# Last block's up products in 2x2 blocks: seven block products in place of eight for three pairs of unit tiles

## The chip, the core and the metric

The kernel runs on one core of a Trainium2 chip. A core has a matmul engine (PE, with its weight loads shown apart as PEld), a vector engine (DVE), an activation engine (ACT), GpSimd (POOL) and a queue engine (SP) that issues most DMA transfers. Each engine carries out its own instructions in order; semaphores tie the engines together. The metric is the device time of one execution in microseconds (us), the median of several runs.

## What is computed

Two branches read the same x (2048 rows, 512 columns) and are mixed row by row by a gate g. Branch A is a linear attention with 32 heads of 16; branch B, where the change lies, is a dense layer of 512 to 1376 units, Mish, and a dense layer back.

```python
g = _sigmoid((x * gate_w).sum(-1, keepdims=True))
a = _A_ref(x, A_wqkv, A_w_phi, A_wo)      # hedgehog features, kv and z sums, o @ wo
# branch B
h = jnp.einsum("bsd,df->bsf", x, w1) + b1
sp = jnp.log1p(jnp.exp(-jnp.abs(h))) + jnp.where(h > 0, h, jnp.zeros_like(h))
act = h * jnp.tanh(sp)
b = jnp.einsum("bsf,fd->bsd", act, w2)
return g * a + (1 - g) * b
```

## The kernel before

**Stages.** A first stage (eight chunks of 256 rows) makes k, v and q, the features of k and the sums over rows. The second stage takes four blocks of 512 rows (`b_ops`), numbered 0 to 3 here, the last being the one that the change touches. A block computes branch B, the features of q, the attention output and the final mix.

**Precision by parts.** A float32 operand is kept as a high part (rounded by ACT into a tile of type F32R) and a low part (operand minus high part, by DVE or POOL). A product is three sums of matmuls: high with high, low with high, high with low. With 512 inputs, four tiles of 128, one product of 128 units by 512 rows is 3 x 4 = 12 matmuls of 512 columns into one PSUM bank.

**The steps of a block.** A block's work is a text of step names; `run` carries them out in the order written, and every instruction is pinned, so each engine meets its part in that order. The names that the prediction uses:

- `up{i}`: the 12 matmuls of hidden tile i (11 tiles of 128 units, the order of the tiles in `ORDER`) into one bank of the PSUM tag "a", which has three banks. `mi{i}`: Mish with bias from that bank on ACT. `hi{i}`: the high part on ACT. `lo{i}`: the low part on POOL.
- `dn{i}`: the second layer's 12 matmuls of tile i (three for each 128 rows), into four banks ("dn") that gather all 11 tiles; `df{t}` is the last tile's share for 128 rows t, `fi{t}` the final mix on DVE and the store.
- `T{t}`, `D{t}` ... `tr{t}`: the attention's features of 128 rows, mostly on DVE; `mv{h}`: 16 small transfers on SP; `nu{h}`: 32 narrow matmuls; `oh{h}`, `ol{h}`: high part of their result on ACT and low part on DVE; `wo{t}`, `ag{t}`: the output product and its scaling by the gate on ACT; `ge`, `gg`: the gate. The Exp of `ge` and Mish need different tables, so ACT loads a table (ACT_TABLE_LOAD) between them.
- `XH{j}`, `XL{j}`: high and low part of the next block's x. A `+` behind a name means the next block's step.

Blocks 2 and 3 run in the order of `BLOCK`, block 3 without the steps marked `+`: ... `up4 mi4 hi4 lo4 dn2 up5 mi5 hi5 lo5 dn3 ge gg wo0 ag0 wo1 ag1 up6 mi6 hi6 lo6 dn4 nu1 oh1 ol1 up7 ... dn5 up8 ... dn6 wo2 ag2 wo3 ag3 up9 ... dn7 up10 ... dn8 dn9 df0 fi0 ...`

**Buffers.** Tiles are taken from tags with a fixed number of buffers: "pq" has 3 (2 KB per partition each), "E" 4, "tx" 2 and "z" 1 (4 KB each), "tt" and "eT" 1 (8 KB each). A new tile of a tag waits until the old one in its buffer has been read for the last time. In the second stage "z" holds the attention's z sums, read for the last time by T3 of block 3.

**An earlier use of the same scheme.** `fast_ops` (lines 355 to 402) already computes some of the first stage's k and q in seven products instead of eight, with the copies and sums on ACT and DVE placed between products of other banks.

Of the kernel before, what the change touches and what calls it, by code (L numbers as in the profile page):

```python
# [10 lines left out]
F32R = mybir.dt.float32r  # L11
# [4 lines left out]
P = 128  # L16
# [16 lines left out]
ORDER = [NFA - 1] + list(range(NFA - 1)) + list(range(NFA, NF))
WARM = 6
FAST = range(2, 6)

# [34 lines left out]
BLOCK0 = """  # L71
# [8 lines left out]
BLOCK1 = """  # L80
# [7 lines left out]
BLOCK = """  # L88
# [1 line left out]
    S3 T3 rS3 D3 m3 de3 rd3 sc3 es3 tr3 lq0+ lq1+ mv1 up3 mi3 hi3 lo3 dn1 up4 mi4 hi4 lo4 dn2  # L90
    mx0+ mn0+ d00+ d10+ mx1+ mn1+ d01+ d11+ lq2+ lq3+ up5 mi5 hi5 lo5 dn3 E0+ E1+ ge gg wo0 ag0 wo1 ag1
    S0+ T0+ rS0+ D0+ m0+ de0+ rd0+ sc0+ es0+ tr0+ up6 mi6 hi6 lo6 dn4 nu1 oh1 ol1 S1+ T1+ rS1+ D1+ LX0 LX1 m1+ de1+ rd1+ sc1+
    es1+ tr1+ mv0+ up7 mi7 hi7 lo7 dn5 mx2+ mn2+ d02+ d12+ mx3+ mn3+ d03+ d13+ up8 mi8 hi8 lo8 dn6 E2+ E3+
    wo2 ag2 wo3 ag3 up9 mi9 hi9 lo9 dn7 up10 mi10 hi10 lo10 dn8 XH0+ XL0+ XH1+ XL1+ dn9 df0 fi0 df1 fi1 df2 fi2 df3 fi3
"""


@with_exitstack
def tile_gated_mix(ctx: ExitStack, tc: tile.TileContext, xT, wv, wkT, wqT, bd, w1a, w1b, b1, w2a, w2b, wo, out):
# [6 lines left out]
    pin = tc.keep_in_program_order  # L106
    SYNC = mybir.DependencyInfo(mybir.DependencyClass.Sync, mybir.DependencyReason.DATA)
    V, G_, A_, Sy = nc.vector, nc.gpsimd, nc.scalar, nc.sync

    def mm(*a, **k):  # L110
        return pin(nc.tensor.matmul(*a, **k))  # L111

    def T(shape, dt, tag, bufs, name):
        nm[0] += 1
        return sp.tile(shape, dt, name=f"{name}_{nm[0]}", tag=tag, bufs=bufs)

    def k8(name, tag, dt=F32R):
        return T([P, 2048], dt, tag, 1, name)

    def k4(name, tag, dt=F32):  # L120
        return T([P, 1024], dt, tag, {"E": 4, "tx": 2, "oh": 2, "z": 1}[tag], name)

    def k2(name, tag, dt=F32):
        return T([P, 512], dt, tag, {"pq": 3, "io": 4, "hl": 8}[tag], name)

    def psum(name, tag, bufs={"a": 3, "dn": 4, "kv": 1}):
        nm[0] += 1
        return pp.tile([P, 512], F32, name=f"{name}_{nm[0]}", tag=tag, bufs=bufs[tag])

    def act(out_, in_, fn=AF.Copy, **k):  # L130
        return pin(A_.activation(out_, in_, fn, **k))  # L131

    def kt(t, f):
        return t[:, : KT * f].rearrange("p (k f) -> p k f", f=f)
# [4 lines left out]
    def f32(ap):  # L139
        return ap.bitcast(F32)  # L140
# [39 lines left out]
    ps = psum("warm", "dn")  # L180
# [79 lines left out]
    def feat_ops(key, t, src, d, negative=False):  # L260

        n = str(t)

        def red(name, op):
            d[name] = T([P, H], F32, name, 2, name)
            pin(V.tensor_reduce(d[name], hv(src()), axis=AX.X, op=op))

        def dd(a):
            if "E" not in d:
                d["E"] = k4("E", "E")  # L270
            E = hv(d["E"][:, a * 512 : (a + 1) * 512])
# [21 lines left out]
    def behind(ins, other=None):  # L293
        tc.add_manual_dep(ins.ins, (other or dve[0]).ins.name, SYNC, reason="VectorE's step first")

    def scale_by(d, eng):
        dve[0] = pin(eng.tensor_mul(hv(d["E"][:, :]), hv(d["E"][:, :]), d["S"][:, :, None].to_broadcast([P, 2 * H, DH])))  # L297
# [33 lines left out]
    def fast_operands(c, key):  # L331
# [12 lines left out]
        for j in range(2):  # L344
# [59 lines left out]
    def a_ops(c):  # L404
        key = ("A", c)
        P_ = psA[c] = {}
        for t in range(2):
# [157 lines left out]
    def wo_ops():
        raw = {}
# [25 lines left out]
    B = {}  # L592
# [43 lines left out]
    def b_ops(b):  # L636
        key = ("B", b)
        U, dn, tts, eTs, num, ohl, io = {}, {}, {}, {}, {}, {}, {}

        def up(i):  # L640
            f = ORDER[i]
            xh, xl = xb[b]
            ps = psum("up", "a")
            n = 0
            for w, a in ((0, xh), (1, xh), (0, xl)):
                for k in range(KT):
                    mm(ps, w1_tile(f, w, k), a[:, k, :], start=(n == 0), stop=(n == 3 * KT - 1))
                    n += 1
            U[i] = {"ps": ps}

        def mi(i):
            f = ORDER[i]
            U[i]["a"] = k2("act", "hl")
            act(U[i]["a"], U[i]["ps"], AF.Mish, bias=b1s[:, f : f + 1])

# [8 lines left out]
        def down(i, t):  # L664
            if t not in dn:
                dn[t] = psum("down", "dn")
            f = ORDER[i]
            h, l = [U[i][x][:, t * P : (t + 1) * P] for x in "hl"]
            for n, (a, x) in enumerate(((h, 0), (h, 1), (l, 0))):
                mm(dn[t], a, w2_tile(f, x), start=(i == 0 and n == 0), stop=(i == NF - 1 and n == 2))  # L670

        for i in range(NF):
            at(key, f"up{i}", lambda i=i: up(i))
            at(key, f"mi{i}", lambda i=i: mi(i))
            at(key, f"hi{i}", lambda i=i: hi(i))
            at(key, f"lo{i}", lambda i=i: lo(i))
            for t in range(4):
                at(key, f"dn{i}" if i < NF - 1 else f"df{t}", lambda i=i, t=t: down(i, t))
# [173 lines left out]
    for j in range(2):  # L852
        h, l = [w[:, 2 * j : 2 * j + 2, :].rearrange("p k f -> p (k f)") for w in (wvh, wvl)]
# [12 lines left out]
    for i in range(4):  # L866
        j, r = i // 2, i % 2
# [27 lines left out]
    for c, text in ((NCH - 2, NEXT), (NCH - 1, LAST)):  # L895
        run(text, ("A", c), ("A", c - 1), ("B", 0))
    for b in range(NB):
        run((BLOCK0, BLOCK1, BLOCK, BLOCK)[b], ("B", b), ("B", b - 1), ("B", b + 1))
    assert not steps, list(steps)


# [58 lines left out]
```

## Time and profile before

| | |
|---|---|
| median of 3 runs | 447.92 us (447.35 to 448.15) |
| the profiled execution's own time | 447.83 us |
| its span, first to last instruction | 446.1 us |
| first stage and start of block 0 (0 to 157) | PE busy 154.45 of 157.00 |
| block 3 and the end (369 to 446.1) | PE busy 73.27 of 77.10, DVE 22.14, ACT 22.82, POOL 14.83 |

The span is what the profile covers; the difference to the execution's time lies outside it. A busy time is the sum of an engine's instructions without overlaps counted twice. Matmuls are pipelined: a recorded 0.39 us for a 512-wide one is its whole passage, while the next one starts 0.2267 us later; the distance between starts (the pitch) is what it costs. The chain that ended last goes back from the last instruction, step by step, to whatever released it, and so names the engine that sets the time in each stretch. In rows of timelines the first number is the start in us from the span's start, the second the length, and brackets tell how long the engine stood idle before and what released it.

### The profile page before, as it was taken

To read this page: it belongs to the slowest core of one execution; us is meant where nothing else is said; L and a number is where in the kernel's file an instruction comes from. 1 tells how busy PE (TensorE), PEld (TensorE's weight loads), DVE (VectorE), ACT (ScalarE), POOL (GpSimd) and SP (SyncE) were. 2 spreads that over 40 slices of the span, in tenths; PEclk is the share of its full clock that TensorE was granted. 3 is DMA by queue.
4 is the path that set the end of the run, shared out by engine and by line. 5 is a ranking of instruction groups with operands and counts; after the bars stand their busy time and mean duration, and the time that the engine had idled before them with its cause. 6 is when DMAs were issued, how large, how long until landed. Compare 5 with 4: busy or idle time off the path is not lost.

```text
span 446.1 us, 7022 instructions
## 1 busy us (share of the span) xinstructions
PE 439.7 (99%) x2748; PEld 359.1 (81%) x2748; DVE 319.6 (72%) x427; ACT 211.3 (47%) x292; POOL 158.9 (36%) x120
## 2 busy tenths in 40 slices
PE   7999999999999999999999999999999999999996
PEld 7888888788888888787878887887887888787885
DVE  2499789888999999799899868386967438701002
ACT  5774644463544837426374443724253544234220
POOL 2297388675666364212023121113202123121211
PEclk9999999999999999999999999999999999999999
DMA  7424559949835111405251241321241302030002
GB/s 281 169 77 160 143 122 233 220 130 312 240 116 166 49 24 32 112 19 148 89 171 49 55 134 48 94 96 47 49 143 48 94 2 95 1 91 5 0 0 94
DMA packets 27320, 46.35 MB, mean 104 GB/s; under 512 B 5908, under 2 KB 14100, under 8 KB 27288
## 3 DMA queue, kind: packets, MB, share of 16 engines
q1 hardware_dynamic: 25528, 39.88, 28.9%
q0 software_dynamic: 1616, 5.77, 6.5%
q8 instruction: 21, 0.34, 0.3%
q10 hardware_dynamic: 144, 0.26, 0.2%
q14 instruction: 11, 0.09, 0.1%
HBM read 23.87 MB, written 13.64 MB: 84 GB/s over the span
## 4 chain that ended last, share of the span: by engine, by line
PE 98%; DMA 1%; DVE 0%; issue 0%
PE proj L111 28%; PE up L111 27%; PE down L111 27%; PE wo L111 10%; PE num L111 2%; PE fuse L111 2%; PE kvp L111 2%; DMA bds<-in_bd_dram 1%; DVE io L797 0%; PE z L111 0%; PE kvT L616 0%
## 5 line engine op out<-in xcount | busy, mean ns | idle before, releaser
L662 POOL TENSOR_TENSOR l<-act,h 128x512 fp32r<-128x512 f32 x44 | 60.4, 1373 | 220.5 <-ACT h L131 184.7
L131 ACT ACTIVATE act<-up,b1s 128x512 f32<-128x512 f32 x44 | 30.3, 689 | 87.4 <-PE up L111 87.3
L131 ACT ACTIVATE E<-E 128x1024 f32<-128x1024 f32 x32 | 33.7, 1060 | 47.9 <-DVE E L275 33.8
L297 DVE TENSOR_TENSOR E<-E,Sm 128x1024 f32<-128x1024 f32 x32 | 42.2, 1320 | 1.0
L281 DVE TENSOR_REDUCE Sm<-E 128x64 f32<-128x1024 f32 x32 | 38.7, 1210 | 4.2 <-ACT E L131 4.2
L111 PE MATMUL wo<-woh,ohl 128*128 128x512 f32 x128 | 40.7, 389 | 0.0
L111 PE MATMUL down<-w2ah,h 128*128 128x512 f32 x96 | 37.5, 390 | 0.0
L111 PE MATMUL down<-w2ah,l 128*128 128x512 f32 x96 | 37.4, 389 | 0.0
L111 PE MATMUL down<-w2al,h 128*128 128x512 f32 x96 | 37.3, 389 | 0.0
L797 DVE SCALAR_TENSOR_TENSOR io<-down,og_sb,io 128x512 f32<-128x512 f32 x16 | 11.1, 748 | 31.0 <-PE down L111 31.0
L111 PE MATMUL down<-w2bh,h 128*128 128x512 f32 x80 | 31.2, 390 | 0.0
L111 PE MATMUL down<-w2bl,h 128*128 128x512 f32 x80 | 31.1, 389 | 0.0
L111 PE MATMUL down<-w2bh,l 128*128 128x512 f32 x80 | 31.1, 389 | 0.0
L131 ACT ACT_TABLE_LOAD x20 | 25.7, 1283 | 10.1 <-PE up L111 9.8
L771 DVE TENSOR_TENSOR ohl<-num,ohl 128x512 fp32r<-128x512 f32 x16 | 10.2, 678 | 26.4 <-ACT ohl L131 26.4
L131 ACT ACTIVATE h<-act 128x512 fp32r<-128x512 f32 x44 | 27.8, 632 | 1.4
L111 PEld LDWEIGHTS wo<-woh,ohl 128*128 128x128 f32 x128 | 24.0, 188 | 5.0
L111 PE MATMUL up<-xbh,w1ah 128*128 128x512 f32 x96 | 26.2, 394 | 0.0
L111 PE MATMUL up<-xbh,w1al 128*128 128x512 f32 x96 | 25.7, 389 | 0.0
L111 PE MATMUL up<-xbl,w1ah 128*128 128x512 f32 x96 | 25.7, 389 | 0.0
L559 DVE TENSOR_TENSOR xbl<-xraw,xbh 128x1024 fp32r<-128x1024 f32 x8 | 10.1, 1290 | 21.0 <-ACT xbh L131 21.0
L111 PE MATMUL wo<-wol,ohl 128*128 128x512 f32 x64 | 24.9, 389 | 0.0
(155 smaller groups left out, 1015.3 us busy)
## 6 DMA issues: line engine op xcount, KB each, us to landing
xraw<-in_xT_dram SPq DMA_DIRECT2D x16, 512.0 KB, 4.6
eT<-tt SPq DMA_DIRECT2D x128, 64.0 KB, 2.0
zd<-E POOLq DMA_DIRECT2D x10, 512.0 KB, 7.4
pqd<-qs SPq DMA_DIRECT2D x16, 256.0 KB, 4.0
pq<-pqd SPq DMA_DIRECT2D x16, 256.0 KB, 2.9
out_dram<-io SPq DMA_DIRECT2D x16, 256.0 KB, 2.1
raw<-in_w1a_dram SPq DMA_DIRECT2D x3, 512.0 KB, 4.2
raw<-in_w2a_dram SPq DMA_DIRECT2D x3, 512.0 KB, 3.6
```

The lines of the kernel that those rows point to most:

```text
L111: return pin(nc.tensor.matmul(*a, **k))
L131: return pin(A_.activation(out_, in_, fn, **k))
L281: pin(V.tensor_reduce(d["S"], hv(d["E"][:, :]), axis=AX.X, op=ALU.add))
L297: dve[0] = pin(eng.tensor_mul(hv(d["E"][:, :]), hv(d["E"][:, :]), d["S"][:, :, None].to_broadcast([P, 2 * H, DH])))
L559: dve[0] = pin(V.tensor_sub(xb[b][1][:, :, sl], kt(raw[h], SC), f32(xb[b][0][:, :, sl])))
L662: pin(G_.tensor_sub(U[i]["l"], U[i]["a"], f32(U[i]["h"])))
L771: pin(V.tensor_sub(ohl[h, gp][:, 512:], num[h, gp], f32(ohl[h, gp][:, :512])))
L797: pin(V.scalar_tensor_tensor(io[t], dn[t], og_sb[:, i : i + 1], io[t], op0=ALU.mult, op1=ALU.add))
```

## The change

In block 3 alone, the tiles at places 5 and 6, 7 and 8, 9 and 10 are computed in pairs. A pair is a product of 256 units by 512 rows over 512 inputs; it is cut in two along each (128 units, 256 inputs, 256 rows), and the eight block products are replaced by seven, with sums made before (of x, of w1) and after (of products), as in Winograd's form of Strassen's scheme. `ORDER3` puts neighbouring tiles of w1 side by side in a pair.

```diff
+ORDER3 = [5, 0, 1, 2, 10, 4, 3, 7, 6, 9, 8]
+PAIRS = (5, 7, 9)
@@ BLOCK
-    ... up8 mi8 hi8 lo8 dn6 E2+ E3+
+    ... up8 mi8 hi8 lo8 dn6 E2+ E3+ X1+ Y0+ Y1+ X2+
+BLOCK3 = """
+    up0 mi0 hi0 lo0 gr S2 T2 rS2 D2 m2 de2 rd2 sc2 es2 tr2 up1 mi1 hi1 lo1 up2 mi2 hi2 lo2 dn0 nu0 oh0 ol0
+    S3 T3 LA5 rS3 D3 m3 de3 rd3 sc3 es3 tr3 mv1 LA7 Y2 Y3 up3 mi3 hi3 lo3 dn1 up4 mi4 hi4 lo4 dn2 CA5 HA5 ge gg wo0 ag0 wo1 ag1
+    f1.5 c1.5 f6.5 c6.5 f2.5 f7.5 c7.5 dn3 f5.5 c5.5 f4.5 c4.5 mi5 hi5 lo5 nu1 oh1 ol1 f3.5 c3.5 mi6 hi6 lo6 dn4 CA7 HA7 LA9
+    f1.7 c1.7 f6.7 c6.7 f2.7 f7.7 c7.7 dn5 f5.7 c5.7 f4.7 c4.7 mi7 hi7 lo7 dn6 f3.7 c3.7 mi8 hi8 lo8 CA9 HA9
+    f1.9 c1.9 f6.9 c6.9 f2.9 f7.9 c7.9 dn7 f5.9 c5.9 f4.9 c4.9 mi9 hi9 lo9 dn8 f3.9 c3.9 mi10 hi10 lo10 wo2 ag2 wo3 ag3
+    dn9 df0 fi0 df1 fi1 df2 fi2 df3 fi3
+"""
+    def x_sums(raw, key):
...
+        def x1():
+            pin(G_.tensor_sub(new(0), quarter(0, 1), quarter(0, 0)))
+            pin(G_.tensor_sub(new(1), quarter(1, 1), t[0]))
+            pin(G_.tensor_sub(new(2), quarter(1, 1), quarter(0, 1)))
+        def x2():
+            pin(G_.tensor_sub(new(3), quarter(1, 0), t[1]))
+        def split(i):
+            q = k4("tq", "tx" if i == 3 else "E", F32R)
+            XT[i] = h, l = [q[:, o : o + 512].rearrange("p (k f) -> p k f", k=2) for o in (0, 512)]
+            act(h, t[i])
+            pin(V.tensor_sub(l, t[i], f32(h)))
...
+    def pair_ops(key, n, f0, f1, U):
...
+        def la():
+            r["t"] = k4("wraw", "z")
+            pin(Sy.dma_start(...))
+        def ca():
+            a11, a12, a21, a22 = [...]
+            pin(V.tensor_add(a22, a21, a22))
+            pin(V.tensor_sub(a21, a11, a21))
+            pin(V.tensor_sub(a11, a22, a11))
+            pin(V.tensor_sub(a12, a12, a11))
+        def ha():
...
+            act(hl[0], r["t"])
+            pin(V.tensor_sub(hl[1], r["t"], f32(hl[0])))
...
+        def term(out_, ws, x, start):
+            m = 0
+            for wi, xi in ((0, 0), (1, 0), (0, 1)):
+                for k in range(2):
+                    mm(out_, ws[wi][k], x[xi][:, k, :], start=(start and m == 0), stop=(m == 5), skip_group_check=True)
+                    m += 1
...
+        def c1():
+            c["a"], c["b"] = k2("c", "pq"), k2("c", "pq")
+            act(c["a"][:, lo], ps[0][:, lo])
+        k0, q0, k1, c22 = [lambda i=i, sl=sl: ps[i][:, sl] for i in range(2) for sl in (lo, hi)]
+        p1, e, u2 = lambda: c["a"][:, lo], lambda: c["a"][:, hi], lambda: c["b"][:, lo]
+        for name, fn in (
+            ("f1", f1_), ("c1", c1),
+            ("f6", lambda: term(q0(), w["s2"], XT[1], False)), ("c6", lambda: add(u2, q0, p1)),
+            ("f2", lambda: term(k0(), plain(f0, 1), rows(1, 0), False)),
+            ("f7", f7), ("c7", lambda: add(e, k1, p1)),
+            ("f5", lambda: term(q0(), w["s1"], XT[0], False)), ("c5", lambda: add(c22, q0, e)),
+            ("f4", lambda: term(k1(), plain(f1, 1), XT[3], False)), ("c4", lambda: add(k1, k1, u2)),
+            ("f3", lambda: term(q0(), w["s4"], rows(1, 1), False)), ("c3", lambda: add(q0, q0, p1)),
+        ):
...
         for i in range(NF):
-            at(key, f"up{i}", lambda i=i: up(i))
+            if last and i >= PAIRS[0]:
+                if i in PAIRS:
+                    pair_ops(key, i, tiles[i + 1], tiles[i], U)
+            else:
+                at(key, f"up{i}", lambda i=i: up(i))
...
-        run((BLOCK0, BLOCK1, BLOCK, BLOCK)[b], ("B", b), ("B", b - 1), ("B", b + 1))
+        run((BLOCK0, BLOCK1, BLOCK, BLOCK3)[b], ("B", b), ("B", b - 1), ("B", b + 1))
```

`BLOCK` now serves block 2 alone; the steps `X1+` to `X2+` exist only for block 3's x.

The parts of a pair, named by the place n of its first tile (`f6.7` is f6 of the pair at 7):

- `LA`: one 512 KB transfer of the two raw tiles of w1, into the one buffer of "z". `CA`: four sums of quarters (128 x 2 x 128) on DVE, each in place and all but the first needing the one before. `HA`: their high part (128 x 1024) on ACT, their low part on DVE.
- `f1` to `f7`: six matmuls of 256 columns each. Two banks serve a pair: f1 and f2 write the lower half of the first, f6, f5 and f3 the upper half; f7 and f4 the lower half of the second, and its upper half is written by DVE alone (c5).
- `c1`: a copy of f1's half on ACT (128 x 256). `c6`, `c7`, `c5`, `c4`, `c3`: sums on DVE (128 x 256). `mi` of the pair's first tile reads the second bank after c4, that of its second tile the first bank after c3.
- `X1`, `X2`: four sums of x for the block on POOL (128 x 512), run in the block ahead of it; `Y0` to `Y3`: their high part on ACT and low part on DVE, two in the block ahead, two in block 3.

The order on **PE** from the last pair but one. Names in a row are out<-in; `up_3888` is a bank, xbh and xbl the parts of x, w1bh and w1bl those of w1, tq a sum of x, ws a sum of w1. Before, the step up7, behind nu1:

```order
L111 MATMUL up_3888<-xbh_3521,w1bh_812 128x512 [waits Activation_49]
L111 MATMUL up_3888<-xbh_3521,w1bh_812 128x512 x3
L111 MATMUL up_3888<-xbh_3521,w1bl_813 128x512 x4
L111 MATMUL up_3888<-xbl_3522,w1bh_812 128x512 x4
L111 MATMUL down_3635<-w2ah_128,h_3783 128x512
```

Now f1, f6 and f2 of the pair at 7, behind dn4 (up_3955 is the pair's first bank):

```order
L121 MATMUL up_3955<-xbh_3535,w1bh_812 128x256 [waits Activation_49]
L121 MATMUL up_3955<-xbh_3535,w1bh_812 128x256
L121 MATMUL up_3955<-xbh_3535,w1bl_813 128x256 x2
L121 MATMUL up_3955<-xbl_3536,w1bh_812 128x256 x2
L121 MATMUL up_3955<-tq_3438,ws_3950 128x256 [waits Activation_49]
L121 MATMUL up_3955<-tq_3438,ws_3950 128x256
L121 MATMUL up_3955<-tq_3438,ws_3950 128x256 [waits DVE_49]
L121 MATMUL up_3955<-tq_3438,ws_3950 128x256 x3
L121 MATMUL up_3955<-xbh_3535,w1bh_812 128x256 [waits DVE_49]
L121 MATMUL up_3955<-xbh_3535,w1bh_812 128x256
L121 MATMUL up_3955<-xbh_3535,w1bl_813 128x256 x2
L121 MATMUL up_3955<-xbl_3536,w1bh_812 128x256 x2
```

Where one step of twelve wide matmuls waited once, three steps of six narrow ones now wait four times: for ACT before f1 and before f6, for DVE at f6's third matmul (the low part of the sums of w1) and before f2.

The order on **DVE** behind nu1. Before, the two ol steps, and then nothing until the final mix:

```order
L771 TENSOR_TENSOR ohl_3882<-num_3864,ohl_3882 128x512 [waits Activation_49]
L771 TENSOR_TENSOR ohl_3884<-num_3865,ohl_3884 128x512 [waits Activation_49]
L797 SCALAR_TENSOR_TENSOR io_3816<-down_3635,og_sb,io_3816 128x512 [waits DMAHW6_49,DVE_49,PE_49]
```

Now c4.5, the two ol steps, c3.5, CA7 (lines 623 to 626), HA7's low part (line 635) and c6.7:

```order
L670 TENSOR_TENSOR up_3857<-up_3857,c_3842 128x256 [waits DVE_49,PE_49]
L900 TENSOR_TENSOR ohl_3915<-num_3897,ohl_3915 128x512 [waits Activation_49]
L900 TENSOR_TENSOR ohl_3917<-num_3898,ohl_3917 128x512 [waits Activation_49]
L670 TENSOR_TENSOR up_3834<-up_3834,c_3841 128x256 [waits PE_49]
L623 TENSOR_TENSOR wraw_3722<-wraw_3722 128x2x128 [waits DMAHW5_49]
L624 TENSOR_TENSOR wraw_3722<-wraw_3722 128x2x128 [waits DVE_49]
L625 TENSOR_TENSOR wraw_3722<-wraw_3722 128x2x128 [waits DVE_49]
L626 TENSOR_TENSOR wraw_3722<-wraw_3722 128x2x128 [waits DVE_49]
L635 TENSOR_TENSOR ws_3950<-wraw_3722,ws_3950 128x1024 [waits DMAHW3_49,DMAHW4_49,DMAHW2_49,DMAHW6_49,DMAHW1_49,DMAHW7_49,DMAHW0_49,Activation_49]
L670 TENSOR_TENSOR c_3963<-up_3955,c_3962 128x256 [waits PE_49,Activation_49]
```

The sums for the second pair stand on DVE behind the first pair's last sum (c3.5) and ahead of the second pair's first (c6.7); those for the third pair stand in the same way between c3.7 and c6.9, without the ol steps.

More of the change, by code (lines that the diff above doesn't have):

```diff
@@ L92 @@
     S0+ T0+ rS0+ D0+ m0+ de0+ rd0+ sc0+ es0+ tr0+ up6 mi6 hi6 lo6 dn4 nu1 oh1 ol1 S1+ T1+ rS1+ D1+ LX0 LX1 m1+ de1+ rd1+ sc1+
-    es1+ tr1+ mv0+ up7 mi7 hi7 lo7 dn5 mx2+ mn2+ d02+ d12+ mx3+ mn3+ d03+ d13+ up8 mi8 hi8 lo8 dn6 E2+ E3+
+    es1+ tr1+ mv0+ up7 mi7 hi7 lo7 dn5 mx2+ mn2+ d02+ d12+ mx3+ mn3+ d03+ d13+ up8 mi8 hi8 lo8 dn6 E2+ E3+ X1+ Y0+ Y1+ X2+
     wo2 ag2 wo3 ag3 up9 mi9 hi9 lo9 dn7 up10 mi10 hi10 lo10 dn8 XH0+ XL0+ XH1+ XL1+ dn9 df0 fi0 df1 fi1 df2 fi2 df3 fi3
+"""
[6 more added lines that the diff above has]
+    dn9 df0 fi0 df1 fi1 df2 fi2 df3 fi3
 """
@@ L563, in x_ops, with quarter, new @@
             at(split, f"XL{h}", xl)
+        if b == NB - 1:
+            x_sums(raw, split)
+    XT = {}
+    def x_sums(raw, key):
+        t = {}
+        def quarter(j, r):
+            return kt(raw[r], SC)[:, 2 * j : 2 * j + 2, :]
+        def new(i):
+            t[i] = k2("traw", "pq")[:, :].rearrange("p (k f) -> p k f", k=2)
+            return t[i]
+        def x1():
[9 more added lines that the diff above has]
+            pin(V.tensor_sub(l, t[i], f32(h)))
+        at(key, "X1", x1)
+        at(key, "X2", x2)
+        for i in range(4):
+            at(key, f"Y{i}", lambda i=i: split(i))
@@ new lines, in pair_ops, with quarter, plain, rows @@
+    def pair_ops(key, n, f0, f1, U):
+        n_, dram, g, nf = ("w1a", w1a, f0, NFA) if f0 < NFA else ("w1b", w1b, f0 - NFA, NFB)
+        r, w, c, ps = {}, {}, {}, {}
+        def quarter(t, i, j):
+            return t[:, 2 * j : 2 * j + 2, i, :]
+        def la():
+            r["t"] = k4("wraw", "z")
+            pin(Sy.dma_start(r["t"].rearrange("p (k m) -> p k m", k=KT), dram.rearrange("p (k m) -> p k m", k=KT)[:, :, g * P : (g + 2) * P]))
+        def ca():
+            a11, a12, a21, a22 = [quarter(r["t"][:, :].rearrange("p (k i f) -> p k i f", k=KT, i=2), i, j) for i in range(2) for j in range(2)]
+            pin(V.tensor_add(a22, a21, a22))
[3 more added lines that the diff above has]
+        def ha():
+            if n == PAIRS[0]:
+                hl = k4("wsh", "E", F32R)[:, :], k4("wsl", "tx", F32R)[:, :]
+            else:
+                t = k8("ws", "tt" if n == PAIRS[1] else "eT")
+                hl = t[:, :1024], t[:, 1024:]
+            act(hl[0], r["t"])
+            pin(V.tensor_sub(hl[1], r["t"], f32(hl[0])))
+            v = [x.rearrange("p (k i f) -> p k i f", k=KT, i=2) for x in hl]
+            for name, i, j in (("s2", 0, 0), ("s4", 0, 1), ("s3", 1, 0), ("s1", 1, 1)):
+                w[name] = [[quarter(x, i, j)[:, k, :] for k in range(2)] for x in v]
+        def plain(f, j):
+            return [[w1_tile(f, x, 2 * j + k) for k in range(2)] for x in range(2)]
+        def rows(j, h):
+            return [x[:, 2 * j : 2 * j + 2, h * SC : (h + 1) * SC] for x in xb[NB - 1]]
+        def term(out_, ws, x, start):
[4 more added lines that the diff above has]
+                    m += 1
+        lo, hi = slice(0, SC), slice(SC, RB)
+        def f1_():
+            ps[0] = psum("up", "a")
+            term(ps[0][:, lo], plain(f0, 0), rows(0, 0), True)
+            U[n + 1] = {"ps": ps[0]}
+        def f7():
+            ps[1] = psum("up", "a")
+            term(ps[1][:, lo], w["s3"], XT[2], True)
+            U[n] = {"ps": ps[1]}
+        def c1():
+            c["a"], c["b"] = k2("c", "pq"), k2("c", "pq")
+            act(c["a"][:, lo], ps[0][:, lo])
+        def add(o, x, y):
+            pin(V.tensor_add(o(), x(), y()))
+        k0, q0, k1, c22 = [lambda i=i, sl=sl: ps[i][:, sl] for i in range(2) for sl in (lo, hi)]
[9 more added lines that the diff above has]
+        ):
+            at(key, f"{name}.{n}", fn)
+        at(key, f"LA{n}", la)
+        at(key, f"CA{n}", ca)
+        at(key, f"HA{n}", ha)
@@ L638, in b_ops @@
         U, dn, tts, eTs, num, ohl, io = {}, {}, {}, {}, {}, {}, {}
+        last = b == NB - 1
+        tiles = ORDER3 if last else ORDER
         def up(i):
-            f = ORDER[i]
+            f = tiles[i]
             xh, xl = xb[b]
@@ L651, in mi @@
         def mi(i):
-            f = ORDER[i]
+            f = tiles[i]
             U[i]["a"] = k2("act", "hl")
@@ L666, in down @@
                 dn[t] = psum("down", "dn")
-            f = ORDER[i]
+            f = tiles[i]
             h, l = [U[i][x][:, t * P : (t + 1) * P] for x in "hl"]
@@ L672, in b_ops @@
         for i in range(NF):
-            at(key, f"up{i}", lambda i=i: up(i))
+            if last and i >= PAIRS[0]:
+                if i in PAIRS:
+                    pair_ops(key, i, tiles[i + 1], tiles[i], U)
+            else:
+                at(key, f"up{i}", lambda i=i: up(i))
             at(key, f"mi{i}", lambda i=i: mi(i))
```

## The prediction

> **What bounds the kernel now.** I read the page first (busy shares, the slices, the chain that ended last), then the chain in order of time through the last block, then the engines' timelines there, and last the groups and tiles for the price of one instruction.
>
> ```profile
> PE 439.7 (99%) x2748; PEld 359.1 (81%) x2748; DVE 319.6 (72%) x427; ACT 211.3 (47%) x292; POOL 158.9 (36%) x120
> PEclk9999999999999999999999999999999999999999
> PE 98%; DMA 1%; DVE 0%; issue 0%
> ```
>
> PE (matmul) is the kernel: 98% of the chain, at full granted clock, waiting for almost nothing. So a matmul taken away is worth its pitch, and every wait put in front of PE costs its full length: nothing else is late enough to absorb it.
>
> ```profile
> 392.06 2.72 PE up L111 x12
> 394.78 2.72 PE down L111 x12
> 397.50 5.44 PE wo L111 x24
> 402.94 2.72 PE up L111 x12
> 405.66 2.72 PE down L111 x12
> 408.38 1.02 PE num L111 x32
> 409.40 2.94 PE up L111 x12
> ...
> 434.11 6.81 PE down L111 x30
> 440.92 0.03 issue
> 440.95 0.69 DVE io L797
> ```
>
> This is the chain through the last block. Twelve 512-wide matmuls take 2.72, a pitch of 0.2267 us, and up, down and wo follow each other without a gap. The 2.94 after num is the one exception (0.22 for refilling). The six up steps touched (the first is at 392.06) cost 6 x 2.72 = 16.32 us.
>
> **The change: the products.** Per pair 2 x 12 matmuls of 512 columns become 7 x 6 of 256. The trace has no 256-wide matmul on the full array with its own weights, so I bound it.
>
> ```profile
> 5.48 4.91 PE L111 MATMUL fuse<-bds,wT 128*128 128x128 f32 x24 [1.43 <-DMA bds<-in_bd_dram]
> 11.61 1.05 PE L111 MATMUL fuse<-bds,wT 128*128 128x128 f32 x8
> L616 PE MATMUL kvT<-ident,km x4: 270/272/273, 162.3 to 162.7; 128*128 128x128 f32 x4
> ```
>
> Eight 128-wide matmuls with new weights each span 1.05; less one's own 0.27 that is 7 pitches of 0.111. That is the floor, set by loading weights. A straight line from 0.111 at 128 columns to 0.2267 at 512 gives 0.150 at 256, the ceiling. If a matmul pays the longer of load and stream, it is about half of 0.2267, 0.113; I take 0.117 (an estimate: half, and a little fixed cost), since the load, 0.111, lies below the half and overlaps. Three pairs: 126 x 0.117 = 14.74, a gain of 1.58 (2.33 at the floor; a loss of 2.58 at the ceiling).
>
> **The change: the trips out of the bank.** The seven products share two PSUM banks, and between them ACT or DVE must read the bank before PE may write it again. In the changed order the row of f6 waits for ACT (c1, which copies f1's half), f2 waits for DVE (c6), and f4 waits for DVE (c5, which writes f4's bank); the waits hold although the other half of the bank is written. Nothing stands between f1 and f6, f6 and f2, or f5 and f4 on PE, so all three trips of a pair are bare. What one costs:
>
> ```profile
> 380.89 1.20 PE L111 MATMUL up<-xbh,w1ah 128*128 128x512 f32 x4
> 381.92 1.07 PE L111 MATMUL up<-xbh,w1al 128*128 128x512 f32 x4
> ...
> 404.59 1.07 PE L111 MATMUL up<-xbl,w1bh 128*128 128x512 f32 x4
> 405.50 0.39 PE L111 MATMUL down<-w2ah,h 128*128 128x512 f32 x1
> ```
>
> ```profile
> 405.74 1.28 ACT L131 ACT_TABLE_LOAD   x1 [2.07 <-PE up L111]
> 407.04 0.69 ACT L131 ACTIVATE act<-up,b1s 128x512 f32<-128x512 f32 x1
> 407.76 0.63 ACT L131 ACTIVATE h<-act 128x512 fp32r<-128x512 f32 x1
> 409.49 1.09 ACT L131 ACTIVATE ohl<-num 128x512 fp32r<-128x512 f32 x2 [1.10 <-PE num L111]
> 410.13 1.29 DVE L771 TENSOR_TENSOR ohl<-num,ohl 128x512 fp32r<-128x512 f32 x2 [11.76 <-ACT ohl L131]
> ```
>
> ```profile
> L131 ACT ACTIVATE ohl<-num x16: 580/596/600, 188.6 to 410.0; 128x512 fp32r<-128x512 f32 x16
> L771 DVE TENSOR_TENSOR ohl<-num,ohl x16: 629/682/692, 190.7 to 410.7; 128x512 fp32r<-128x512 f32 x16
> L736 DVE TENSOR_TENSOR Dn<-Dn,Sm x16: 224/226/1307, 158.7 to 386.8; 128x64 f32<-128x64 f32 x16
> L131 ACT ACTIVATE ge_sb<-ge_sb 128x4 f32<-128x4 f32 x1 | 0.2, 205 | 0.0
> L131 ACT ACTIVATE xbh<-xraw 128x1024 fp32r<-128x1024 f32 x2 | 2.0, 1044 | 0.0
> 387.93 1.23 DVE L297 TENSOR_TENSOR E<-E,Sm 128x1024 f32<-128x1024 f32 x1
> ```
>
> PE's slot ends when its next piece starts, 405.50; ACT starts at 405.74: 0.24 later. DVE comes 0.03 after the recorded end (440.92 to 440.95), and a recorded end lies 0.16 behind its slot (405.66 against 405.50): 0.20. ACT to DVE is 0.04 (409.49 + 0.60 to 410.13); I use 0.04 for every hand-over, also back to PE. A PE that had to wait then pays a weight load that nothing hides: after num, four matmuls take 381.92 - 380.89 = 1.03 where four pitches are 0.91, so 0.12. Widths: DVE 0.226 at 64 and 0.682 at 512, so 0.42 at 256; ACT 0.205 at 4 and 0.596 at 512, so 0.40 (bounds: half of, and all of, the 512 price). A trip by ACT is 0.24 + 0.40 + 0.04 + 0.12 = 0.80, by DVE 0.20 + 0.42 + 0.04 + 0.12 = 0.78. Of nine trips two (f1 to f6 of the second and third pair) drown in the longer wait below. The other seven: 0.80 + 6 x 0.78 = 5.48 us lost.
>
> **The change: the sums of w1.** For the second and third pair four dependent adds (CA), a rounding on ACT and a subtraction on DVE (HA) stand on DVE behind c3 of the pair before, and f6 needs their result. Each add is 0.42 + 0.04, HA 1.05 on ACT and 1.22 on DVE (rows above).
>
> Third pair, from the end of f3.7: 0.20 + c3 0.42 + 0.03 + adds 1.84 + 0.04 + 1.05 + 0.04 + 1.22 + 0.04 = 4.88 until f6.9's third matmul (first with low weights) may go. PE's only cover is f1.9, 0.70, and two matmuls, 0.23. With one bare load (0.12): 4.07 lost.
>
> Second pair, from the end of f4.5: 0.20 + c4 0.42, then ACT 0.04 + table load 1.28 + mi 0.71 + hi 0.66 + oh's two 1.12, then DVE 0.04 + last ol 0.65 + 0.03 + c3.5 0.42 + adds 1.84, then 0.04 + 1.05 + 0.04 + 1.22 + 0.04 = 9.80. c3.5 is ready early but queued behind ol, which waits for ACT, whose table load waits for c4. PE's cover: nu 1.02 + 0.22, f3.5 0.70, dn4 2.72, f1.7 0.70, two matmuls 0.23 = 5.59. With one bare load: 4.33 lost.
>
> First pair: its sums stand behind T3 and the last transpose, and wo0 and wo1 (5.44) follow before f1.5, so they are covered.
>
> ```profile
> 373.35 1.29 POOL L662 TENSOR_TENSOR l<-act,h 128x512 fp32r<-128x512 f32 x1 [9.58 <-ACT h L131]
> 373.68 1.05 DVE L736 TENSOR_TENSOR Dn<-Dn,Sm 128x64 f32<-128x64 f32 x1
> ```
>
> DVE's 64-wide product of two SBUF tensors, 0.226 when alone, took 1.05 and ended with POOL's subtraction: one of them waits for the other. In both chains the low part (lo6, lo8) becomes ready about 0.1 after the fourth add has started (1.41 against 1.52 after c3), waits for it, and then holds HA's subtraction up to 1.87 + 1.29 = 3.16 instead of 3.00: 0.16 each, 0.32. If POOL wins that race the add waits instead, about 1.1 more per pair. [...]
>
> **What is covered.** Four more POOL subtractions and two splits for x run in block two, where POOL has nothing between the low parts:
>
> ```profile
> 346.16 1.30 POOL L662 TENSOR_TENSOR l<-act,h 128x512 fp32r<-128x512 f32 x1 [4.15 <-ACT h L131]
> 358.32 1.29 POOL L662 TENSOR_TENSOR l<-act,h 128x512 fp32r<-128x512 f32 x1 [10.86 <-ACT h L131]
> raw<-in_w1a_dram SPq DMA_DIRECT2D x3, 512.0 KB, 4.2
> ```
>
> 10.86 idle against 4 x 1.3. The other two splits run on ACT and DVE before up3's Mish. The three loads of 512 KB take about 4.2: the first leaves after T3, the second when the first HA ends (about 396, needed at 412), the third after the second HA (10 before its use). On SP they are ahead only of transfers needed later. Without that cover a load would add up to 4.2.
>
> **The sum:** -1.58 + 5.48 + 4.33 + 4.07 + 0.32 = +12.6 us. On the profiled execution's 447.83 (span 446.1, the rest lies outside and stays; the median of the runs is 447.92): **460.4 us**, 2.8% slower.
>
> **Rivals.** (a) *The trips are not bare*: PE runs on into the other half of the bank and the weights are ready, so only the 1.58 is left: 446.3, faster. It would need eight of the nine trips, and both sums of w1, hidden. For it: nothing on DVE is busy late (3 tenths and less in the last slices). Against: waits in the changed order, and DVE's strict order. (b) *Only the trips cost*: the sums of w1 get done in time, nine trips 7.0 - 1.6: 453.3. Against: c3 is ahead of the adds. (c) *PE comes back slow* after two idle stretches of some 4 us. For it: at the start, after 1.43 idle, 24 of the fuse matmuls took 4.91, 0.20 each, against 0.111 later. Such a stretch loses (0.20 - 0.111) x 24 = 2.2; one or both: 462.6 to 464.8. Against: PE is never idle long in the rest of the trace, so no row shows it after warm work. [...]
>
> **The numbers.** Forecast 0.72, (c) 0.14, (b) 0.09, (a) 0.04, something within 0.2% 0.01; 0.2% (0.9 us) is what a measurement of this kernel can tell from no change. Low end: narrow steps at half the 512 price take off 1.5 and the floor pitch 0.75, so 458.2, and I go on to 456.5, part of the way to (b). High end: the pitch at 0.150 adds 4.2, or (c) adds 2.2 to 4.4: 464.5. Narrow steps at the full 512 price, or two lost races with POOL, land within that too. Faster 0.04, same 0.01, slower 0.95.
>
> **What would show it.** In the changed trace PE's idle time should show two stretches near 4 us ahead of f6 of the second and third pair, released by HA's parts, and seven of 0.6 to 0.9 ended by ACT c1 once and DVE c6 and c5 six times; starts of 256-wide matmuls 0.11 to 0.12 apart; PE clock at full. PE running f6 right after f1 would prove me wrong, as would adds of CA that start before c3, or a pitch near 0.15.

## The result

| | before | after |
|---|---|---|
| median | 448.03 us (447.32 to 449.0, 6 runs) | 466.66 us (465.19 to 468.31, 6 runs) |
| the profiled execution's own time | 447.83 us | 467.42 us |
| its span | 446.1 us | 465.7 us |

The ratio (of the means, here and below) is 1.0414, with a 95% interval of 1.0384 to 1.0443: slower, as forecast, but by 18.6 us and not by 12.6, and 2.2 us above the range. The forecast and every step behind it stood for a full clock; the third rival, PE coming back slow, is what happened.

The same three lines of the page, now of after (busy shares, granted clock by slices, chain that ended last):

```profile
PE 447.4 (96%) x2802; PEld 366.3 (79%) x2802; DVE 339.1 (73%) x461; ACT 216.9 (47%) x302; POOL 165.2 (35%) x124
PEclk9999999999999999999999999999999999997799
PE 93%; DVE 3%; ACT 1%; DMA 1%; issue 0%; DVEq 0%; ACTq 0%
```

PE has 54 matmuls more (126 narrow ones for 72), and its share falls from 99 to 96%. In the chain DVE rises from 0 to 3% and ACT comes in with 1%, and two slices show a clock of 0.7. The waits of PE in the last block, in a view that lists who ended them (us in all, how many, the longest):

```profile
PE up L121 <- ACT c L141: 6.9, 3, 3.1
PE up L121 <- DVE c L670: 1.8, 3, 0.6
PE up L121 <- DVE up L670: 1.6, 3, 0.5
PE up L121 <- DVE ws L635: 0.7, 2, 0.5
```

Before, this view is empty for the last block. Nine trips (three each by c1, c6 and c5) and two waits for the low weights of the sums of w1: the waits the prediction named, at the places it named. "ACT c" holds both c1 of the first pair and the two long stretches, because c1.7 and c1.9 stand on ACT behind the rounding of the sums, and PE needs both.

PE's timeline around the second pair (start, length, instruction, in brackets the idle time before it and its releaser), f1.7 first:

```profile
413.34 0.40 PE L121 MATMUL up<-xbh,w1bh 128*128 128x256 f32 x2
413.57 0.40 PE L121 MATMUL up<-xbh,w1bl 128*128 128x256 f32 x2
413.81 0.40 PE L121 MATMUL up<-xbl,w1bh 128*128 128x256 f32 x2
417.30 0.51 PE L121 MATMUL up<-tq,ws 128*128 128x256 f32 x2 [3.09 <-ACT c L141]
418.28 1.22 PE L121 MATMUL up<-tq,ws 128*128 128x256 f32 x4 [0.48 <-DVE ws L635]
...
421.54 1.48 PE L121 MATMUL up<-tq,ws 128*128 128x256 f32 x6
422.82 0.63 PE L121 MATMUL down<-w2ah,h 128*128 128x512 f32 x1
423.25 0.63 PE L121 MATMUL down<-w2al,h 128*128 128x512 f32 x1
...
426.48 0.87 PE L121 MATMUL up<-tq,ws 128*128 128x256 f32 x6
```

Two matmuls of f1.7 take 0.235, so a pitch of 0.118. f7 at 421.54 takes 422.82 - 421.54 = 1.28 for six, 0.213 each, and the 512-wide ones after it start 0.43 apart in place of 0.2267. By 426.48 six take 0.87 of passage again. PE runs at half pace for some microseconds behind the pause. The view of stretches shows it as the granted clock. The edges here are those at which the trace's clock changes, carried on in steps of 3.41 us; the columns are the stretch, its length, the busy time of PE, PEld, DVE, ACT and POOL with their instructions, the granted clock, and the DMA's share and GB/s:

```profile
397.45:400.87 3.42, 2.50 (x15) 2.04 (x14) 1.33 (x4) 2.60 (x5) 0.00 (x0) 1.00 0.40 97
400.87:404.28 3.41, 2.82 (x21) 2.53 (x21) 0.79 (x2) 0.00 (x0) 0.00 (x0) 1.00 0.46 88
...
414.52:417.93 3.41, 0.51 (x2) 0.30 (x2) 2.20 (x4) 2.40 (x4) 1.27 (x1) 1.00 0.00 0
417.93:421.35 3.42, 2.48 (x10) 2.19 (x11) 0.72 (x2) 0.00 (x0) 0.00 (x0) 0.50 0.37 115
421.35:424.76 3.41, 3.41 (x13) 3.02 (x13) 0.42 (x1) 0.00 (x0) 0.00 (x0) 0.50 0.11 38
424.76:428.17 3.41, 2.89 (x16) 2.35 (x16) 0.43 (x1) 0.00 (x0) 0.00 (x0) 1.00 0.00 0
431.59:435.00 3.41, 1.44 (x13) 1.23 (x11) 2.03 (x5) 1.80 (x3) 1.24 (x2) 1.00 0.00 0
435.00:438.41 3.41, 2.02 (x6) 1.43 (x6) 1.41 (x2) 0.85 (x2) 0.62 (x1) 0.50 0.00 0
438.41:441.83 3.42, 3.13 (x13) 3.06 (x14) 0.40 (x2) 0.00 (x0) 0.00 (x0) 0.50 0.00 0
```

After each of the two long pauses the clock is 0.50 for 6.83 us, two steps of 3.41. The step ahead of the first had PE busy for 0.51 of 3.41; that ahead of the second for 1.44, so it was 42% busy, and the clock fell all the same. The other five runs were not profiled, but none was spared: the mean clock of all six is 0.982 to 0.989, against 1.000 in the profiled execution before.

**Where the 19.6 us of the two profiled executions lie** (467.42 - 447.83). From the end of dn2, behind which the orders differ, to the last matmul it is 17.3 longer. The last matmul starts at 441.88 before and at 460.70 after; from its end to the end of the span it is 3.83 before and 4.60 after, 0.8 more. The other 1.5 is there before the orders differ, and 1.15 of it by 13 us, where the change has no instruction. The start, of after:

```profile
5.77 5.49 PE L121 MATMUL fuse<-bds,wT 128*128 128x128 f32 x24 [1.71 <-DMA bds<-in_bd_dram]
```

Before, these 24 matmuls began at 5.48 and took 4.91. The trace's clock turns full at 9.6 before and at 11.7 after; in the eight other profiled executions of this study (the kernels below) it did so between 4.0 and 10.4. It differs with the execution, not with the change.

### The profile page after: what moved, and what is told of

Same layout as the page of the kernel before. It is cut to its first block, busy times and chain, and to the rows that moved or that the text cites. A ratio compares the mean times of both kernels' runs of the same rounds, so it can differ in the third digit from the quotient of the medians.

```text
span 465.7 us, 7209 instructions
## 1 busy us (share of the span) xinstructions
PE 447.4 (96%) x2802; PEld 366.3 (79%) x2802; DVE 339.1 (73%) x461; ACT 216.9 (47%) x302; POOL 165.2 (35%) x124
## 4 chain that ended last, share of the span: by engine, by line
PE 93%; DVE 3%; ACT 1%; DMA 1%; issue 0%; DVEq 0%; ACTq 0%
PE proj L121 27%; PE up L121 26%; PE down L121 25%; PE wo L121 9%; PE fuse L121 2%; PE kvp L121 2%; PE num L121 2%; DMA bds<-in_bd_dram 1%; DVE io L926 1%; DVE up L670 1%; DVE ws L635 1%; ACT ws L141 0%; DVE c L670 0%; DVE ohl L900 0%; ACT L141 0%
## 5 line engine op out<-in xcount | busy, mean ns | idle before, releaser
L121 PE MATMUL up<-xbh,w1ah 128*128 128x512 f32 (+1 forms) x92 | 25.1, 392 | 0.6 <-DVE c L670 0.6
L121 PE MATMUL up<-xbh,w1al 128*128 128x512 f32 (+1 forms) x92 | 24.4, 385 | 0.0
L121 PE MATMUL up<-xbl,w1ah 128*128 128x512 f32 (+1 forms) x92 | 24.3, 384 | 0.0
L900 DVE TENSOR_TENSOR ohl<-num,ohl 128x512 fp32r<-128x512 f32 x16 | 10.2, 679 | 17.9 <-ACT ohl L141 17.9
L859 DVE STREAM_TRANSPOSE tt<-E 128x1024 f32<-128x1024 f32 x16 | 19.9, 1246 | 3.3 <-DMA eT<-tt 2.7
```

Of the source, the lines that this page charges most:

```text
L859: pin(V.transpose(tts[h][:, t % 2, :, :].rearrange("p k x -> p (k x)"), d["E"][:, :]))
L900: pin(V.tensor_sub(ohl[h, gp][:, 512:], num[h, gp], f32(ohl[h, gp][:, :512])))
```

## The experiments

Each kernel below was run against the kernel before on the same chip; the change's own 466.66 is from the runs of the result, where the kernel before took 448.03 (447.5 to 448.0 in those below).

**The late sums alone: `e1_early`.** The sums of w1 for the second and third pair stand ahead of the oh, ol and c3 they were queued behind; all nine trips stay bare.

```diff
-... c4.5 mi5 hi5 lo5 nu1 oh1 ol1 f3.5 c3.5 mi6 hi6 lo6 dn4 CA7 HA7 LA9
-f1.7 c1.7 f6.7 ... c4.7 mi7 hi7 lo7 dn6 f3.7 c3.7 mi8 hi8 lo8 CA9 HA9
+... c4.5 CA7 mi5 hi5 lo5 nu1 f3.5 c3.5 HA7 oh1 ol1 dn4 LA9
+f1.7 c1.7 mi6 hi6 lo6 f6.7 ... c4.7 CA9 mi7 hi7 lo7 dn6 HA9 f3.7 c3.7
```

> The sums of w1 for the second and third pair are taken earlier (behind c4 of the pair before), the trips out of the bank stay. Theory A (late sums make PE wait, and the long wait makes the granted clock fall): both waits of 4.0 to 4.3 us and both slow stretches (together 4.4 us) are gone, clock 1.00 in all windows; nine bare trips of 0.8 less 1.2 for the products leave 448 + 6 = 454 us (453 to 455). Theory B (the clock falls for the narrow matmuls or their load, not for the idle time): windows below 1.00 stay, 458 to 459 us. Theory C (the sums are late anyway, since DVE is the bound): 460 or more.

Measured: 455.5 us (454.92 to 456.04), ratio 1.0175 (1.0156 to 1.0194), 11.2 below the change and 0.5 above the range of theory A. Its waits:

```profile
PE up L121 <- ACT c L141: 1.9, 3, 0.9
PE up L121 <- DVE c L670: 1.8, 3, 0.6
PE up L121 <- DVE up L670: 1.6, 3, 0.5
```

The three c1 now wait 1.9 in all and not 6.9, the row of ws is gone, and the granted clock is 1.00 in the whole block. Nine trips with their bare weight loads come to 7.6 (0.74 to 0.85 each, the first 1.19). So the order of the sums is worth more than the 8 us of the two pauses, although two trips that had drowned in them (1.5) now count; what it is worth beyond them is the next experiment's.

**The clock alone: `e2_fill13`.** The waits stay, but PE is kept busy through the two pauses with 13 matmuls of 512 columns whose result nobody reads.

```diff
+        def fill():
+            ps[1] = psum("up", "a")
+            for _ in range(13):
+                mm(ps[1], w1_tile(f0, 0, 0), xb[NB - 1][0][:, 0, :], start=True, stop=True)
...
-f1.7 c1.7 f6.7 ...
+f1.7 c1.7 fill.7 f6.7 ...
...
```

> The change with 13 matmuls of 512 columns that nothing reads, put between f1 and f6 of the second and third pair, where PE stands idle for 3 us; nothing else moved. Theory A: the waits end when they ended before, but PE is busy through them, so the clock stays at 1.00 and only the slow stretches go: 466.7 - 4.4 = 462 us (461 to 463). Theory B: windows near 0.5 stay and the time stays at 466 to 468.

Measured: 461.67 us (461.16 to 461.89), ratio 1.0309 (1.0294 to 1.0324). The second pair again, in PE's timeline:

```profile
412.66 3.14 PE L121 MATMUL up<-xbh,w1bh 128*128 128x512 f32 x13
415.89 0.50 PE L121 MATMUL up<-tq,ws 128*128 128x256 f32 x2
416.88 0.74 PE L121 MATMUL up<-tq,ws 128*128 128x256 f32 x4 [0.49 <-DVE ws L635]
...
419.02 0.88 PE L121 MATMUL up<-tq,ws 128*128 128x256 f32 x6
```

f6's third matmul still starts 4.94 behind the start of f1.7, as in the change, but f7 takes 0.88 in place of 1.48, and the granted clock is 1.00 from 397 to 441 us. Work that computes nothing made the kernel 5.0 us faster. The half clock of the change (0.50 for 6.83 us behind each pause) is thus shown to come from PE's idle time, and to cost about what the change loses beyond its waits.

**How much idle time it takes: `e6_fill5`.** The same with 5 such matmuls.

> The change with 5 unread 512-wide matmuls (5 x 0.227 = 1.1 us) between f1 and f6 of pairs 7 and 9, so that about 2 us of each stretch stays idle in place of 3.1 to 3.3. Theory A (the clock halves wherever some 55 to 60 per cent of a 3.4 us window of the gate is idle, as in e5_one): half clock in most runs, time between e2_fill13's 461.7 and the change's 466.7, about 464 to 466. Theory B (it takes a stretch near 3 us without a matmul): clock full, 461 to 463, and the spread of runs under 1.5 us.

Measured: 466.12 us (465.72 to 467.44), ratio 1.0425 (1.0409 to 1.0441): nothing gained on the change, and every run below full clock (0.985 to 0.989 on the mean). Stretches of the profiled execution in the same steps:

```profile
397.05:400.46 3.41, 1.90 (x14) 1.49 (x13) 0.43 (x1) 1.12 (x3) 0.00 (x0) 1.00 0.40 96
400.46:403.88 3.42, 3.42 (x14) 3.03 (x13) 0.42 (x1) 0.00 (x0) 0.00 (x0) 0.50 0.57 173
...
431.18:434.60 3.42, 2.35 (x15) 1.78 (x14) 2.04 (x5) 2.06 (x3) 1.25 (x2) 1.00 0.00 0
434.60:438.01 3.41, 1.70 (x9) 1.29 (x10) 1.65 (x2) 0.59 (x2) 0.37 (x1) 1.00 0.00 0
438.01:441.42 3.41, 3.41 (x15) 3.12 (x14) 0.42 (x1) 0.00 (x0) 0.00 (x0) 0.50 0.00 0
```

A step with PE busy for 1.70 or 1.90 of 3.41 is followed by half clock here; one with 2.35 is not. Theory B falls. The first two rows are a surprise: there no long pause stands, only the first pair's two short trips, both inside one step. In the change the same two trips fell into two steps (2.50 and 2.82 busy, above), and the clock stayed.

**One pair only: `e5_one`.** `PAIRS = (5,)`; the tiles at 7 to 10 are plain again, so that no sum of w1 is late.

> Only the first pair (places 5 and 6) is done in seven products, the other four tiles by plain up steps; the sums of x stay. Its sums of w1 are in time. Theory A: three trips of 0.8 to 1.1 (2.8) less a third of the products' gain (0.4): 448 + 2.4 = 450.4 us (449.7 to 451), clock 1.00. If a pair costs more than its trips (the sums of x in the block ahead, the loads, a shift in the first stage): 451.5 or more.

Measured: 451.43 us (449.62 to 452.7, 4 runs), ratio 1.0079 (1.0055 to 1.0102), above the range of theory A. Two of the four runs, 451.69 (the profiled one) and 452.7, had a mean clock of 0.994, the other two, 449.62 and 451.17, a full one. The profiled one:

```profile
397.17:400.58 3.41, 1.90 (x14) 1.49 (x13) 0.42 (x1) 1.33 (x3) 0.00 (x0) 1.00 0.43 103
400.58:404.00 3.42, 3.42 (x15) 3.13 (x14) 0.42 (x1) 0.00 (x0) 0.00 (x0) 0.50 0.08 19
```

Short trips alone can halve the clock, when two of them share a step. By the mean clocks, whether they do differs with the execution, and the time with it (means of 452.2 and 450.4, of two runs each); that this is the whole miss is not shown.

**All waits covered: `e3_cover`.** e1 with dn3, dn5 and dn7 cut in halves and set between f1 and f6 and between f5 and f4, and f7 set ahead of f2.

```diff
...
-f1.7 c1.7 mi6 hi6 lo6 f6.7 c6.7 f2.7 f7.7 c7.7 dn5 f5.7 c5.7 f4.7 c4.7 ...
+f1.7 c1.7 mi6 hi6 lo6 dn5.0 dn5.1 f6.7 c6.7 f7.7 c7.7 f2.7 f5.7 c5.7 dn5.2 dn5.3 f4.7 c4.7 ...
...
```

> As the run with early sums, and the trips are covered too: half of a dn step between f1 and f6 and between f5 and f4, and f7 between f6 and f2. Theory A: no wait over 0.2 us left on PE in block 3, only the gain of the products stands: 448 - 1.2 = 446.8 us (446.3 to 448). If trips or sums hide something else (a bank, ACT's order), it stays at 449 or more.

Measured: 447.57 us (447.12 to 448.85, 12 runs) against 447.95 (17 runs), ratio 0.9999 (0.9988 to 1.001): no different from before. The chain of the second pair and the end:

```profile
408.75 0.71 PE up L121 x6
409.46 1.39 PE down L121 x6
410.85 2.99 PE up L121 x24
413.84 1.39 PE down L121 x6
```

No wait is left: PE alone, six matmuls in 0.71 or 24 in 2.99. But the products' gain does not show in the time. From the end of dn2 to the last matmul it is 49.31 against 49.98 before: 0.67 gained, the pitch's 1.2 less some bare loads of 0.10. And the end of the span gives it back: 4.61 from the end of the last matmul, in place of 3.83.

**The end of the span: `e7_turn` and `e8_turned`.** In the change as in e3 the last stores are issued as early behind the last matmul as before, but the end comes later. At the end SP waits for eight semaphores of its transfers, in both traces in the same turn. Before, the last four stores have the last four places of this turn, and in the change, with three more loads ahead of them, the last and the first three. Before, the last store lands at 445.18 and SP's wait for it, the eighth, ends at 445.23; in the change it lands at 464.04, and the waits behind its own, the third, last until 464.77. e7 is e3 with the three loads cut into eight transfers, a whole turn; e8 is the kernel before with one load of x cut into four.

```diff
...
+            cut = (0, 2, 4) if n == PAIRS[0] else (0, 1, 2, 4)
+            for a, z in zip(cut, cut[1:]):
-            pin(Sy.dma_start(r["t"]..., ...))
+                pin(Sy.dma_start(r["t"]...[:, a:z, :], ...))
```

> e3_cover with the three loads of w1's pairs cut into eight transfers (2, 3 and 3) in place of three; nothing else differs. In the runs so far the time from the end of the last matmul to the end of the span was 3.83 us before, 4.37 with one load added, 4.60 with three added, whatever lay ahead of it; SyncE's waits at the end stand in a fixed turn of eight semaphores, and the added loads move the last stores to the front of that turn (stores on turns 5 to 8 before, on 8, 1, 2 and 3 with three loads more). Theory A (the tail is the turn): eight loads bring the stores back to turns 5 to 8, the tail is 3.8 again, and the time falls by 0.8 on e3_cover to 446.8 (446.2 to 447.3), ratio 0.997 to 0.999. Theory B (the tail comes with the added instructions or the larger code): tail 4.6, time 447.6, no different from before.

> The kernel before with its last load of x cut into four transfers of one k-tile each, so that three transfers are added long ahead of the end and nothing of the change is in it. Theory A (the tail is the turn of the stores among the semaphores): tail 4.6 in place of 3.83, time 448.7 (448.3 to 449.2), ratio 1.001 to 1.003. Theory B (the tail comes with the change's instructions): tail 3.83, time 447.9, ratio 1.000.

Measured, from the end of the last matmul to the end of the span: e7 3.94, e8 4.28. Times: e7 447.47 us (446.57 to 448.75, 11 runs), ratio 0.9997 (0.9986 to 1.0008); e8 447.92 us (447.18 to 449.24, 12 runs), ratio 1.0011 (0.9998 to 1.0023); the kernel before 447.6 in that job. With the stores back in their old places e7's end is 0.67 shorter than e3's, and three more transfers lengthen the end of a kernel that has nothing of the change by 0.45. So the turn is a cause of the longer end, for 0.45 (e8) to 0.67 (e7); what makes up the rest of the 0.78 stays open. These are single executions, but the end is 4.59 to 4.61 in all six with three loads more (the change, e1, e2, e3, e6, e9). e8's end fell short of the 4.6 forecast for it, and its time of the 448.7. In the times neither is separable from no change, and the forecast of 446.8 for e7 was not borne out.

**The first trip: `e9_c1first`.** The change with c1.5 ahead of ag1 on ACT (`wo1 f1.5 c1.5 ag1`).

> The change with one step moved on ACT: c1.5 ahead of ag1 (wo1 f1.5 c1.5 ag1). In the change the first trip, f1.5 to f6.5, took 1.08 to 1.19 in place of the 0.80 forecast; there c1 stood behind ag0 and ag1, which waited together for the gate, and the gate came behind the sums of the first pair, whose first add took 1.51 beside a POOL subtraction in place of 0.42. Theory A (c1 is late by the queue on ACT): the pause of PE between f1.5 and f6.5 falls by about 0.4, to 0.7 to 0.8, c1 starts within 0.3 of f1's end, and the span up to f6.5 is 0.4 shorter. Theory B (the trip by ACT simply costs 1.1 to 1.2 after a chain of 512-wide products): the pause stays above 1.0. The time itself, 465.5 to 467.5, tells nothing, because the start of a run alone moves it by more.

Measured (one execution, 463.23 us). PE's timeline at f6.5, first of the change, then of e9:

```profile
399.30 0.40 PE L121 MATMUL up<-xbl,w1ah 128*128 128x256 f32 x2
400.62 0.51 PE L121 MATMUL up<-tq,wsh 128*128 128x256 f32 x2 [0.92 <-ACT c L141]
```

```profile
397.25 0.40 PE L121 MATMUL up<-xbl,w1ah 128*128 128x256 f32 x2
398.12 0.51 PE L121 MATMUL up<-tq,wsh 128*128 128x256 f32 x2 [0.47 <-ACT c L141]
```

1.32 from start to start becomes 0.87, 0.45 less: theory A. With a bare load the trip is 0.74 in place of 1.19. It is one execution, but the pause, 0.92 or 0.93, stands in e1, e2, e5 and e6 too, where c1 is behind ag1.

The rest of the 4.2 between the two profiled executions has other sources. dn2 ends 2.05 earlier in e9 (391.50 against 393.55), most of that at the start, and the half clock lasted one step of 3.41 us behind each of the two pauses, and not two. The steps ahead of the first pause of e9 also show that the limit is not sharp:

```profile
410.16:413.57 3.41, 1.56 (x10) 1.23 (x8) 3.12 (x7) 1.82 (x4) 1.11 (x2) 1.00 0.00 0
413.57:416.98 3.41, 1.24 (x6) 0.83 (x6) 1.58 (x2) 1.17 (x2) 0.95 (x1) 1.00 0.00 0
416.98:420.40 3.42, 3.30 (x14) 3.20 (x15) 0.40 (x2) 0.00 (x0) 0.00 (x0) 0.50 0.52 153
```

PE was busy for 1.56 in the first of them and the clock stayed full for the next; it fell only after 1.24. That is less than the 1.70 and 1.90 that halved it in e5 and e6.

## Why the prediction was right and wrong

**The products: forecast -1.58, measured -1.2.** The pitch is 0.118 in f1.7 above and 0.12 over most of the block, against 0.117: 126 x 0.12 = 15.1 in place of 16.32. The row used for the pitch, half of 0.2267 with a little, was nearly right.

**The trips: forecast 5.48, measured 6.1 at full clock.** The trips by DVE cost 0.79 to 0.85 against 0.78. The first by ACT cost 1.19 against 0.80. "First pair: its sums stand behind T3 ... so they are covered" was wrong by 0.4: they were done in time for f6, but the gate, ag0 and ag1 stand behind them on ACT, and c1 behind these. Why the gate was late is read from two rows of after (argued; no run takes the collision away):

```profile
392.41 1.84 POOL L787 TENSOR_TENSOR l<-act,h 128x512 fp32r<-128x512 f32 x1 [4.20 <-ACT h L141]
393.02 1.51 DVE L623 TENSOR_TENSOR wraw<-wraw 128x256 f32<-128x256 f32 x1
```

The first add of CA5 took 1.51 in place of 0.42 beside POOL's subtraction. The prediction had priced such a wait, 0.32, for the two later pairs, where the subtraction of HA now starts 0.02 behind ACT's rounding, with nothing in between; it struck the first pair. The add took the same 1.51 in e1, e2, e3, e5, e6 and e7. In e9 the race went the other way: POOL's subtraction took 1.29, the split of x ahead of the sums was held in the add's place, and the add took its 0.41:

```profile
389.80 2.39 DVE L602 TENSOR_TENSOR tq<-traw,tq 128x512 fp32r<-128x512 f32 x2
392.12 0.41 DVE L623 TENSOR_TENSOR wraw<-wraw 128x256 f32<-128x256 f32 x1
```

The gate came equally late, with ag0 starting 5.68 behind wo0's first matmul against 5.64, so DVE's queue lost about 1.1 in both (1.51 against 0.42 here, 2.39 against 1.25 for the two splits in e9), whichever of its instructions met the subtraction. What the prediction read from one row of before, 1.05 against 0.226, is thus shown again, but not at the place I expected.

**The late sums: forecast 4.33 and 4.07, measured about 4.1 and 3.9.** From the start of f1.7 to f6.7's third matmul it is 418.28 - 413.34 = 4.94; eight pitches of 0.118 would be 0.95; 3.99 with no bare load counted, 4.1 with one. The third pair by the same rows (432.15 and 436.89) gives 3.79 and 3.9. The queue on DVE (c3 behind ol, the four adds behind c3) was read rightly, and e1, which changes that queue and with it ACT's order (HA's rounding ahead of oh, Mish of the pair's second tile behind c1), takes both pauses away.

**The sum at full clock: forecast +12.6, measured 12.9.** -1.2 + 6.1 + 8.0.

**The step that failed is the weight given to rival (c):** a chance of 0.14, and with it a forecast at full clock. That two pauses of some 4 us would most likely leave the clock full was my estimate, and no row of before showed it. The runs show that a partly idle step suffices: every step at full clock with PE busy for 1.44 of 3.41 or less was followed by 0.50, and none with 2.35 or more in this block. In between it went either way (1.70 and 1.90 fell, e9's 1.56 did not). A pause of 4 us takes 2 us or more out of one step of 3.41, wherever the steps fall, and leaves PE 1.41 or less there; so by what the runs show the rival was close to certain once two such pauses were forecast. The steps keep one grid in after: the five changes of the clock between 11.7 and 441.8 lie 119, 2, 3 and 2 steps of 3.413 apart. The size came out right: 2.2 for each stretch, 4.4 for both, stands against 17.3 - 12.9 = 4.4, and e2 gives 5.0 for the whole. Part of that is luck: the 2.2 was the price of 24 matmuls at the kernel's start, and how long the clock stays halved (two steps each in after, one each in e9) was not forecast. Ranking it first would have given 464.8, still 1.9 low and already above the 464.5 at which the stated range ended.

**What no step named:** the longer end, 0.8. It lies inside the span, and the sum has no term for it. Of the 1.5 at the start, the part by which one execution differs from another belongs in no forecast of the median. 12.9 + 4.4 + 0.8 + 1.5 makes the 19.6.

**Rivals (a) and (b)** fall by the list of waits: PE does not run on into the bank's other half (nine trips), and the sums are late. (b)'s own situation is e1, whose 455.5 lies 2.2 above the 453.3 given for it: trips of 7.6 and not 7.0, the products' 1.2 and not 1.6, and the longer end are most of it.

## What to carry to other kernels

A wait put in front of a matmul engine that never rests cost its own length here and then, once the engine was busy for 1.44 us or less of a step of 3.41 (and at times for 1.70 or 1.90), half the pace for the next 3.4 or 6.8: price both, and where a pause can't be avoided, put other work of the engine into it, even work that computes nothing, and enough of it (13 matmuls gained 5.0 us here, 5 gained nothing). Saving one product in eight was worth 1.2 us of 16 here, because a 256-wide matmul cost more than half a 512-wide one (0.12 against 0.2267); each trip through another engine cost 0.74 to 0.85 (the first 1.19), so that two bare trips undo a pair's gain of 0.4 several times over. Of a moved step, follow what stands behind it on its engine (here the gate and c1), and count transfers too: three more made the end of a kernel 0.45 longer here (e8).

## What the runs showed of the hardware that was not expected

- The granted clock fell after a partly idle step. In the last block a step of 3.41 us at full clock with PE busy for 1.44 or less was always followed by half clock, one with 2.35 or more never; between them 1.70 (e6) and 1.90 (e5, e6) were, 1.56 (e9) and, at the end of the kernel, 1.62 (e6) and 1.90 (e1) were not. What decides there is open; the edges of the steps are taken from the trace's clock.
- At half clock it returned to full after a step in which PE was busy for 2.86 (e9), 3.13 (the change) or more, and stayed at half for another step after 2.02 and 2.48 (the change) and 2.82 (e6).
- Where the steps fall differed between the profiled executions: the first pair's two trips halved the clock where both fell into one step (e5, e6; PE busy for 1.90 of 3.41), and left it full where they fell into two (the change; 2.50 and 2.82). In e9 both fell into one step too, but the first was 0.45 shorter, PE was busy for 2.35, and the clock stayed full.
- The moment at which the clock first turns full differed from 4.0 to 11.7 us between profiled executions, and the start of the first 64x64 matmul behind it from 15.9 to 17.9.
- The end of the span differed with the places of the last four stores in the turn of eight semaphores: 3.83 (before) and 3.94 (e7) in the last four places, 4.28 (e8) and 4.59 to 4.61 (three loads more) in the last and the first three.
